# Attention and two mixture-of-experts layers on one core: the first layer in three token passes instead of four

## The chip, the core and the metric

The program runs on one core of a Trainium2 chip. The core has five engines with instruction queues of their own: TensorE (PE; its weight loads are shown apart as PEld), VectorE (DVE), ScalarE (ACT), GpSimd (POOL) and SyncE (SP, which here only issues transfers). They meet through semaphores. The metric is the device time of one launch in microseconds, lower is better. Before the change it is 1419.59 us, the median of 3 runs (1416.87 to 1421.7).

## What is computed

Four batches of 576 tokens go through block-causal attention with 8 heads, then through two feed-forward layers. All is float32, cut here to what matters:

```python
# attention: q, k, v are (4 batches, 8 heads, 576 tokens, 64)
scores = q @ k.T / 8, masked where block_of(query) < block_of(key)   # blocks of 64
x = softmax(scores) @ v                          # -> (2304 tokens, 512)
# first layer ("moe1"): w_gate, w_val (512, 1536), w_out (1536, 512)
x = (1 / (1 + exp(-(x @ w_gate))) * (x @ w_val)) @ w_out
# second layer ("moe2"): 4 experts, w1 (512, 1024), w2 (1024, 512) each
p = domain_probs / (sum(domain_probs) + 1e-9)
out = sum over e of p[:, e] * (relu(x @ w1[e]) @ w2[e])
```

## The kernel before

**Precision and products.** A float32 operand is split in two fp32r tiles, a high part (made on ACT) and a remainder (made on DVE or POOL), and each product is three matmuls: high by high, high by low, low by high. On top of that the products with `w_gate`/`w_val` and `w1` are done in seven block products instead of eight, over two token halves `t`, two column blocks and two halves of the contraction. The sums that this needs are prepared by POOL: for the tokens in `winograd_left` (tiles `xs`, then seven tiles `xc1[1]` to `xc1[7]`), for the weights in `conv_items` (tiles `wa` to `wd`).

**First layer.** The 2304 tokens are taken in passes; before the change four passes of one batch each (`NP1`, `TP1`), so that each matmul streams half a pass, `TH1` = 288 token columns. In a pass a loop runs over 12 slices `f` of 128 of the 1536 hidden columns. For each `f`, `l1_1` does seven products of six matmuls each in two PSUM banks, `c1` and `c2`: ACT copies partial sums out (`snap`), DVE adds them up (`total`), the gate is made by ACT and DVE, and the result is split in the tile `g`. For each two slices, `l2_1` multiplies `g` with `w_out` (tile `wo`), into bank `lo`: 4 blocks `dm` of 128 output columns by 2 token halves, each group 6 matmuls in a row; ACT or DVE adds the group to the tile `x2[t, dm]`, and after the last two slices it is written to DRAM (`x2_d`). A pass has 12 x (42 + 24) = 792 matmuls. The products `l1_1` of two slices and `l2_1` of the two slices before them are merged in one list by cost.

**Weights.** They come as 64-bit floats. In the stretch before the first pass and in pass 0, `conv_items` and `wo_get` convert and split them (ACT, DVE and POOL) and write the split form to DRAM; every later pass loads it again, per slice 4 transfers for `wa` to `wd` and one for `wo`.

**Attention** is a list of items (`attn_items`) put in between: `attn_to` advances it while the first layer runs, to a place set by `A1` and `PACE1`. Batches 0 and 1 ("N") use plain float32 matmuls, 2 and 3 ("F") the split form. Each pair of heads of a batch gives two DRAM tiles: `xd..a`, tokens 0 to 255, and `xd..b`, tokens 256 to 575. They are read back by `x1_prep` or `x1_early` to make the seven token tiles of a pass. While attention runs it owns the PSUM banks `s`, `t` and `o`; from pass 2 on, where it is over, `m_bank` gives the first layer these too, so each of `c1`, `c2` and `lo` has two banks, and the gate is a plain sigmoid.

**Second layer.** Three passes of 768 tokens (`TH` = 384 columns per matmul). In its pass 0 the second matmul has 512 columns, in passes 1 and 2 it is again in seven products, with 256 columns. Its first weights (`w_prep`, `w_load`, `w2_load`) and first token tiles (`x_prep(0)`) are made during the last pass of the first layer.

**Order.** The program is emitted in the order of these lists; a scheduler then moves instructions within each engine by a timeline of its own, and a pool's `bufs` number says how many tiles of a name live at once. SP carries all large transfers in one queue, in order.

Of the kernel before, what the change touches and what calls it, by code (L numbers as in the profile page):

```python
# [21 lines left out]
A1 = [1.05, 2.3, 4, 4, 4]  # L22
PACE1 = 0.9
GB = 4
UB = 1
# [9 lines left out]
W2B = 4  # L35
FIRSTP = 1
W1B = 5
PRE0, PRE1 = 0.4, 0.9
# [24 lines left out]
def attention_moe_moe_kernel(  # L63
# [72 lines left out]
    moe1 = tc.alloc_tile_pool(name="moe1", bufs=1)  # L136
# [15 lines left out]
    def attn_items(segs):  # L152
# [6 lines left out]
        QTS = KTS = {"N": range(5), "F": range(5)}  # L159

        def nat_of(g):
            return pairs[g][3] != "F"
# [20 lines left out]
        def load(g, nm, src, c0, c1):  # L183
# [14 lines left out]
            for x, (y, z) in enumerate(((nm, src),) if nm == "v" else (("k", k), ("q", q)) if nm == "k" else ()):  # L198
                nc.sync.dma_start(
                    out=t[64 * x:64 * x + 64, 4], in_=z[b, 2 * pr:2 * pr + 2, 512:S, :].rearrange("h p d -> p h d"))  # L200
# [6 lines left out]
        def loads(g):  # L207
            load(g, "q", q, 0, 4)
# [61 lines left out]
        first = sum(x[3] != "F" for x in pairs)  # L270
# [4 lines left out]
        for g, pair in enumerate(pairs):  # L275
# [3 lines left out]
            if pair[3] == "F":  # L279
# [10 lines left out]
        order = {"N": 0, "F": 0}  # L290
# [251 lines left out]
        def prep_list(g):  # L542
            seg = pairs[g][3]
            r = [(False, 0.0, lambda: prep_alloc(g))]
            for nm, cs in (("q", range(4)), ("k", KTS[seg])):
# [12 lines left out]
        for g in range(len(pairs)):  # L558
# [5 lines left out]
            later(base + per // 2, (g, False, 0.0, lambda g=g: load_v(g)))  # L564
# [47 lines left out]
    NP1 = B  # L612
    TP1 = S
    TH1 = TP1 // 2
    QF = 2 * P
    KH = NKT // 2
    C1 = TH1 / 2.4 + 2.6
# [3 lines left out]
    wo_d = [dram.tile([P, 2, DM], F32, name=f"wod{i}") for i in range(NF)]  # L621
# [3 lines left out]
    def w1_tile(k):  # L625
        n = 1 if k == "d" else 2
        return moe1.tile([P, 2, n, QF], F32R, tag="wd" if k == "d" else "wg", name=f"w{k}", bufs=2 if k == "d" else 6)
# [48 lines left out]
    def wo_get(p, f):  # L676
        t = wo[f] = moe1.tile([P, 2, DM], F32R, tag="wo", name="wo", bufs=4)
        if p:
            nc.sync.dma_start(out=t.bitcast(F32), in_=wo_d[f])
# [3 lines left out]
        split_sb(t[:, 0], t[:, 1], from_f64(raw), "a", "p")  # L683
        nc.sync.dma_start(out=wo_d[f], in_=t.bitcast(F32))
# [18 lines left out]
    def winograd_left(pool, dst, load, n):  # L703
# [7 lines left out]
        def s(kk, m):  # L711
            if m in (1, 3):
                d[kk, "s", m] = pool.tile([P, n], F32, tag=f"xs{m}", name="xs")
# [22 lines left out]
    def x1_prep(p):  # L736
        def load(kk, t, h):
            kt = h * KH + kk
            r = moe1.tile([P, TH1], F32, tag="xr1", name="xr1", bufs=4)
            while (p, "b", kt) not in x_d:  # L740
                attn_next()
            if t == 0:
                nc.sync.dma_start(out=r[:, :QA], in_=x_d[p, "a", kt])
# [690 lines left out]
```

## Time and profile before

| | us |
|---|---|
| median of 3 runs | 1419.59 (1416.87 to 1421.7) |
| the profiled execution | 1417.34 |
| its span, first to last instruction | 1415.6 |
| busy in the span: PE / DVE / ACT / POOL | 1373.8 / 983.1 / 780.7 / 480.4 |
| attention alone with weight conversion | 0 to about 117 |
| first layer, passes 0 and 1, attention beside them | about 117 to 470 |
| first layer, passes 2 and 3 | about 470 to 680.5 |
| second layer, passes 0, 1, 2 | 680.5 to 930, to 1160, to 1415.6 |

The span is what one execution shows on the engines; 1.7 us lie around it. A matmul's own duration in the profile contains the way through the array, which the next one overlaps, so what a matmul costs in a stream is read from the distance of starts, not from its duration.

### The profile page before, as it was taken

To read this page: it belongs to the slowest core of one execution; us is meant where nothing else is said; L and a number is where in the kernel's file an instruction comes from. 1 tells how busy PE (TensorE), PEld (TensorE's weight loads), DVE (VectorE), ACT (ScalarE), POOL (GpSimd) and SP (SyncE) were. 2 spreads that over 40 slices of the span, in tenths; PEclk is the share of its full clock that TensorE was granted. 3 is DMA by queue.
4 is the path that set the end of the run, shared out by engine and by line. 5 is a ranking of instruction groups with operands and counts; after the bars stand their busy time and mean duration, and the time that the engine had idled before them with its cause. 6 is when DMAs were issued, how large, how long until landed. Compare 5 with 4: busy or idle time off the path is not lost.

```text
span 1415.6 us, 26232 instructions
## 1 busy us (share of the span) xinstructions
PE 1373.8 (97%) x9212; PEld 1266.7 (89%) x9212; DVE 983.1 (69%) x2103; ACT 780.7 (55%) x1926; POOL 480.4 (34%) x502
## 2 busy tenths in 40 slices
PE   5889999999999999999999999999999999999998
PEld 3447788889899999999999989989999999999998
DVE  6867789986766445467777666757766687766766
ACT  5878788888876433343445445445444454443442
POOL 4544345312112100012576556533322342322322
PEclk8989999999999999999999999999999999999999
DMA  7988787767756888898799888886676777676754
GB/s 227 311 243 277 218 278 264 246 204 214 217 178 229 306 296 267 282 364 311 264 336 358 296 300 302 281 308 227 226 254 249 249 266 278 246 269 231 276 205 157
DMA packets 213683, 371.93 MB, mean 263 GB/s; under 512 B 75568, under 2 KB 140080, under 8 KB 207408
## 3 DMA queue, kind: packets, MB, share of 16 engines
q1 hardware_dynamic: 212464, 369.99, 77.1%
q8 instruction: 74, 1.21, 0.3%
q14 instruction: 57, 0.47, 0.1%
q10 hardware_dynamic: 1088, 0.26, 0.1%
HBM read 269.00 MB, written 101.19 MB: 262 GB/s over the span
## 4 chain that ended last, share of the span: by engine, by line
PE 83%; DMA 5%; DVE 5%; ACT 3%; issue 2%; SPq 1%; POOL 1%; DVEq 0%; ACTq 0%; POOLq 0%
PE c L119 37%; PE o L119 25%; PE lo L119 7%; PE s L119 4%; PE obank L119 3%; PE t L119 2%; PE tbank L458 2%; DMA raw<-in_moe_w_out_dram 1%; DMA raw<-in_moe_w_gate_dram 1%; PE s L349 1%; DMA wa<-w1d 1%; ACT pt L382 1%; DMA w1g<-w1d 1%; PE tbank L229 1%; POOL wt L653 1%
## 5 line engine op out<-in xcount | busy, mean ns | idle before, releaser
L119 PE MATMUL c<-xc,w1g 128*128 128x384 f32 x1920 | 384.8, 338 | 2.1 <-DMA w1g<-w1d 1.8
L119 PEld LDWEIGHTS c<-xc,w1g 128*128 128x128 f32 x1920 | 330.4, 188 | 8.8 <-DVE hb L1062 1.3
L119 PE MATMUL o<-w2s,hb 128*128 128x256 f32 x1728 | 243.5, 282 | 1.1 <-DVE acc L1211 1.1
L119 PEld LDWEIGHTS o<-w2s,hb 128*128 128x128 f32 x1728 | 231.8, 189 | 2.0 <-DVE acc L1211 1.7
L1211 DVE SCALAR_TENSOR_TENSOR acc<-o,pr_t,acc 128x256 f32<-128x256 f32 x264 | 123.4, 479 | 57.9 <-PE o L119 55.7
L1071 POOL TENSOR_TENSOR hs<-hf 128x384 f32<-128x384 f32 x64 | 64.1, 1023 | 287.1 <-ACT hf L1079 255.7
L119 PE MATMUL lo<-g,wo 128*128 128x288 f32 x888 | 148.0, 300 | 4.8 <-DVE x L884 4.8
L119 PE MATMUL o<-w,hb 128*128 128x512 f32 x576 | 142.9, 391 | 0.0
L119 PEld LDWEIGHTS lo<-g,wo 128*128 128x128 f32 x888 | 125.8, 188 | 9.6 <-DVE x L884 6.7
L1079 ACT ACTIVATE hf<-c 128x384 f32<-128x384 f32 x128 | 65.7, 513 | 115.7 <-DVE c L1116 58.4
L119 PEld LDWEIGHTS o<-w,hb 128*128 128x128 f32 x576 | 107.2, 188 | 18.5 <-DVE acc L1155 0.3
L1116 DVE TENSOR_TENSOR c<-c,snap 128x384 f32<-128x384 f32 x144 | 77.9, 553 | 55.8 <-PE c L119 38.9
L1109 ACT ACTIVATE snap<-c 128x384 f32<-128x384 f32 x144 | 65.8, 485 | 85.6 <-PE c L119 85.4
L1060 ACT ACTIVATE hb<-hs 128x384 fp32r<-128x384 f32 x128 | 63.3, 518 | 65.0 <-POOL hs L1071 64.9
L1062 DVE TENSOR_TENSOR hb<-hs,hb 128x384 fp32r<-128x384 f32 x128 | 87.1, 695 | 5.8 <-ACT hb L1060 5.4
L884 DVE TENSOR_TENSOR x<-lo,x 128x288 f32<-128x288 f32 x124 | 55.6, 452 | 45.6 <-PE lo L119 45.0
L119 PE MATMUL c<-xc,wa 128*128 128x288 f32 x504 | 82.6, 299 | 0.9 <-DMA wa<-w1d 0.5
L382 ACT ACTIVATE pt<-s,nm 128x128 f32<-128x128 f32 (+3 forms) x128 | 67.4, 530 | 17.2 <-DVE nm L380 14.5
L119 PEld LDWEIGHTS c<-xc,wa 128*128 128x128 f32 x504 | 71.2, 188 | 3.1 <-DMA wa<-w1d 0.8
L119 PE MATMUL c<-xc,wc 128*128 128x288 f32 x432 | 71.0, 299 | 1.1 <-ACT snap L808 1.1
L458 PE MATMUL tbank<-ident,pt 128*128 128x128 f32 x320 | 55.3, 287 | 17.2 <-ACT pTa L445 9.9
L808 ACT ACTIVATE snap<-c 128x288 f32<-128x288 f32 x108 | 44.2, 409 | 43.8 <-PE c L119 43.2
(173 smaller groups left out, 2697.5 us busy)
## 6 DMA issues: line engine op xcount, KB each, us to landing
w1g<-w1d SPq DMA_DIRECT2D x96, 512.0 KB, 5.4
w2s<-w2d SPq DMA_DIRECT2D x48, 1024.0 KB, 6.5
w1d<-w1g SPq DMA_DIRECT2D x48, 512.0 KB, 5.0
wa<-w1d SPq DMA_DIRECT2D x40, 512.0 KB, 5.2
wb<-w1d SPq DMA_DIRECT2D x40, 512.0 KB, 5.3
wc<-w1d SPq DMA_DIRECT2D x40, 512.0 KB, 4.4
wo<-wod SPq DMA_DIRECT2D x36, 512.0 KB, 6.0
wr<-in_moe_w_dram SPq DMA_DIRECT2D x32, 512.0 KB, 5.4
```

Of the source, the lines that this page charges most:

```text
L119: ins = nc.tensor.matmul(out=out, lhsT=lhsT, rhs=rhs, start=start, stop=stop, skip_group_check=skip)
L382: ins = nc.scalar.activation(out=pt[:, x * nk:(x + 1) * nk], in_=sp[:, x - x0], func=AF.Exp, bias=nm[:, j0 + x:j0 + x + 1], scale=1.0, acc ...
L458: nc.tensor.transpose(out=tbank[:, x * P:(x + 1) * P], in_=pt[:, x * P:(x + 1) * P], identity=ident)
L808: nc.scalar.activation(out=t, in_=d["c1"][:, :TH1], func=AF.Copy)
L884: nc.vector.tensor_tensor(out=x2[t, dm], in0=ps, in1=x2[t, dm], op=ALU.add)
L1060: nc.scalar.activation(out=t[:, 0], in_=src, func=AF.Copy if low is None else AF.Relu)
L1062: nc.vector.tensor_tensor(out=t[:, 1], in0=src, in1=t[:, 0].bitcast(F32), op=ALU.subtract)
L1071: nc.gpsimd.tensor_tensor(out=o, in0=x, in1=y, op=op)
L1079: nc.scalar.activation(out=hf[q, blk], in_=c, func=AF.Relu)
L1109: nc.scalar.activation(out=t, in_=d["c1"][:, :TH], func=AF.Copy)
L1116: nc.vector.tensor_tensor(out=c, in0=d[tag][:, :TH], in1=d[n], op=ALU.add)
L1211: nc.vector.scalar_tensor_tensor(out=o, in0=ps, scalar=pr, in1=o, op0=ALU.mult, op1=ALU.add)
```

## The change

The first layer takes three passes, of 576, 832 and 896 tokens, so that its matmuls stream 288, 416 and 448 columns. That has consequences in three places.

*Tokens.* Pass 1 consists of batch 1 and the first 256 tokens of batch 2, pass 2 of the rest of batch 2 and batch 3 (table `X1`). So that the first 256 tokens of batch 2 are there in time, the attention of batch 2 is two segments, "G" (query tiles 0 and 1 of every head pair) and "H" (tiles 2 to 4); key tiles 0 and 1 are loaded and transposed in both. `A1` and `PACE1` place batch 1 and G in pass 0, H and batch 3 in pass 1. The two-bank form holds for the last pass only.

*Space.* The one pool `moe1` becomes pools per pass (`mg`, `mx`, `my`) and one for the weights (`wts`), released and opened again between passes. There are 5 weight tiles instead of 6 (`WGB`), `wo` comes in halves of which 6 are held (3 whole ones, 4 before), 2 `snap` tiles instead of 3 (`SNB`). Raw token loads and sums use tiles that the gate uses later (`room`). `l2_1` goes over `dm` first and the token half second.

*Seams.* After pass 0 its last `l2_1` list is emitted before anything of pass 1 (`go(prev, [])`). The token tiles of pass 2 lie where attention lay, and are made during the last two slices of pass 1 (`XE`). At the end of the first layer one part of the weights of slice 0 of the second layer and all weights of its slice 1 are prepared after the last `l2_1` list (`run(wp[0][6:7] + wp[1])`); before, all but three parts were made inside the last pass.

```diff
-A1 = [1.05, 2.3, 4, 4, 4]
-PACE1 = 0.9
+A1 = [1.05, 3.05, 5, 5]
+PACE1 = (1.0, 0.9, 0.9)
+WGB = 5
+WOB = 6
+SNB = 2
+XE = 2
...
-        QTS = KTS = {"N": range(5), "F": range(5)}
+        QTS = {"N": range(5), "F": range(5), "G": range(2), "H": range(2, 5)}
+        KTS = {"N": range(5), "F": range(5), "G": range(2), "H": range(5)}
...
-    NP1 = B
-    TP1 = S
-    TH1 = TP1 // 2
+    N1 = (288, 416, 448)
+    O1 = (0, 576, 1408)
+    NP1 = len(N1)
+    X1 = (((0, "a", 0, 256), (0, "b", 0, 32)), ((0, "b", 32, 320),)), \
+         (((1, "a", 0, 256), (1, "b", 0, 160)), ((1, "b", 160, 320), (2, "a", 0, 256))), \
+         (((2, "b", 0, 320), (3, "a", 0, 128)), ((3, "a", 128, 256), (3, "b", 0, 320)))
...
     def x1_prep(p):
+        n = N1[p]
+        keep = {}
+
+        def room(key, m):
+            if key not in keep:
+                pool, tag = (xst, key[0]) if p == 2 else (my[p], key[0])
+                keep[key] = pool.tile([P, m, n], F32, tag=tag, name="xr1", bufs=dict(c=2, snap=SNB).get(tag, 1))
+            return keep[key]
...
+            for b, g, c0, c1 in X1[p][t]:
+                while (b, g, kt) not in x_d:
+                    attn_next()
+                nc.sync.dma_start(out=r[:, o:o + c1 - c0], in_=x_d[b, g, kt][:, c0:c1])
+                o += c1 - c0
...
         def snap(n):
-            t = d[n] = moe1.tile([P, TH1], F32, tag="snap", name="snap", bufs=3)
+            t = d[n] = my[p].tile([P, n1], F32, tag="snap", name="snap", bufs=SNB)
...
-        for t in (1, 0):
-            for dm in range(NKT):
+        for dm in range(NKT):
+            for t in (1, 0):
...
-                    pre = x_prep(0) + [...] + wp[0] + wp[1][:-2] + [...]
+                    pre = x_prep(0) + [...] + wp[0][:6] + wp[0][7:] + [...]
...
+                    if p == 1 and f >= NF - XE:
+                        if f == NF - XE:
+                            attn_to(99)
+                            xcp[2] = tc.alloc_tile_pool(name="xc2", bufs=1, side="right", reuse_waits="tile")
+                            xst = tc.alloc_tile_pool(name="xst", bufs=1, side="right", reuse_waits="tile")
+                            xi = x1_prep(2)
+                        x0 = f - (NF - XE)
+                        side += [x for _, x in xi[len(xi) * x0 // XE:len(xi) * (x0 + 1) // XE]]
...
                 prev = l2_1(p, f0)
+                if f0 == NF - 2 and p < NP1 - 1:
+                    my[p].release()
+                    mx[p].release()
+                    if p == 0:
+                        go(prev, [])
+                        prev = []
+                        mg[0].release()
...
         run(prev)
         ps1.release()
-        moe1.release()
-        p2 = tc.alloc_tile_pool(name="p2", bufs=1, reuse_waits="tile")
+        mg[2].release()
+        xcp[2].release()
+        wts.release()
+        p2 = tc.alloc_tile_pool(name="p2", bufs=1, side="right", reuse_waits="tile")
         ps2 = tc.alloc_tile_pool(name="ps2", bufs=1, space=PSUM, reuse_waits="tile")
+        hb_first = [p2.tile([P, 2, TH], F32R, tag="hb", name="hb", bufs=HB)]
         w2_load(1)
+        run(wp[0][6:7] + wp[1])
```

**TensorE between pass 0 and pass 1.** `lo` is the bank of `l2_1`, `c_..` a bank of `l1_1`, `xc_..` a token tile, `tbank`, `s` and `obank` are attention. Before, where the first products of pass 1 (`xc_3697`, `xc_3705`) begin:

```order
L478 MATMUL tbank<-ident,pt_4093 128x128 x4
L119 MATMUL lo<-g,wo 128x288 x6
L119 MATMUL c_3754<-xc_3697,wa 128x288 x6
L119 MATMUL c_3808<-xc_3705,wa 128x288 x3
L119 MATMUL s<-tk,tq 128x128
```

And of the change, the same place (pass 1 has 416 columns):

```order
L512 MATMUL tbank<-ident,xr 128x128 x2
L514 MATMUL tbank<-ident,nm 128x128
L124 MATMUL c_4008<-xc_3952,wa 128x416 x3
L124 MATMUL c_4044<-xc_3960,wa 128x416 x3
L124 MATMUL c_4008<-xc_3952,wa 128x416
L124 MATMUL lo<-g,wo 128x288 x6
L124 MATMUL c_4044<-xc_3960,wa 128x416
```

In both, products of pass 1 stand between the last groups of pass 0. In the change the first two products are cut in pieces of 3, 1 and 2 matmuls, each of which waits for a part of the token tiles, and seven more `lo` groups of pass 0 and the attention of batch 2 follow before the third product.

**ScalarE at the start of the second layer.** `w_9286`, `w_9306` and `w_8203`, `w_8211` are the high parts of the first two down-projection weights, made from raw tiles `wr_..`; `snap` frees a partial sum of the first products; before:

```order
L1109 ACTIVATE snap<-c_9269 128x384
L912 ACTIVATE w_9286<-wr_9089 128x512
L912 ACTIVATE w1g<-wt 128x512
L912 ACTIVATE w_9286<-wr_9089 128x512
L1121 ACTIVATE hb<-c 128x384
L1109 ACTIVATE snap<-c_9339 128x384
L912 ACTIVATE w_9306<-wr_9267 128x512 x2
L1109 ACTIVATE snap<-c_9269 128x384
```

And of the change:

```order
L920 ACTIVATE w1g<-wt 128x512
L920 ACTIVATE w1g<-wr_7798 128x512
L1139 ACTIVATE snap<-c_8194 128x384
L920 ACTIVATE w_8203<-wr_7988 128x512 x2
L1151 ACTIVATE hb<-c 128x384
L920 ACTIVATE w_8211<-wr_8167 128x512 x2
L1139 ACTIVATE snap<-c_8257 128x384
L1139 ACTIVATE snap<-c_8194 128x384
```

Two weight copies for slices 0 and 1 stand ahead of the first `snap`, and both later `snap` copies stand behind `w_8211`; before, one of them stood ahead of `w_9306`.

**TensorE at the same place.** The bank `c_9269` (`c_8194` in the change) is used by the first product, and again by three later ones of the same slice, each of which waits for a `snap`; before:

```order
L119 MATMUL c_9269<-xc_8150,w1g 128x384 x6
L119 MATMUL c_9294<-xc_8239,w1g 128x384 x6
L119 MATMUL c_9316<-xc_8221,w1g 128x384 x6
L119 MATMUL c_9339<-xc_8150,w1g 128x384 x6
L119 MATMUL c_9428<-xc_8221,w1g 128x384 x6
L119 MATMUL c_9269<-xc_8270,w1g 128x384 x6
L119 MATMUL c_9378<-xc_8239,w1g 128x384 x6
L119 MATMUL c_9269<-xc_8339,w1g 128x384 x6
```

And of the change:

```order
L124 MATMUL c_8194<-xc_7107,w1g 128x384 x6
L124 MATMUL c_8219<-xc_7152,w1g 128x384 x6
L124 MATMUL c_8246<-xc_7138,w1g 128x384 x6
L124 MATMUL c_8257<-xc_7107,w1g 128x384 x6
L124 MATMUL c_8194<-xc_7238,w1g 128x384 x6
L124 MATMUL c_8296<-xc_7152,w1g 128x384 x6
L124 MATMUL c_8194<-xc_7267,w1g 128x384 x6
```

The third use of that bank is the eighth product before and the seventh now.

Over the whole program the change has 792 matmuls fewer in the first layer and 8 transposes of keys more.

## Rows read from the trace of the kernel before

**Rows 1.** The page: busy time and share of the span by engine.

```profile
PE 1373.8 (97%) x9212; PEld 1266.7 (89%) x9212; DVE 983.1 (69%) x2103; ACT 780.7 (55%) x1926; POOL 480.4 (34%) x502
```

**Rows 2.** The page: the chain of work that ended last, by engine.

```profile
PE 83%; DMA 5%; DVE 5%; ACT 3%; issue 2%; SPq 1%; POOL 1%; DVEq 0%; ACTq 0%; POOLq 0%
```

**Rows 3.** Stretches: PE, PEld, DVE, ACT, POOL busy (instructions); clock, DMA, GB/s.

```profile
207.00:297.00 90.00, 84.02 (x605) 73.98 (x603) 82.90 (x201) 76.78 (x212) 38.67 (x39) 1.00 0.79 254
297.00:440.00 143.00, 142.67 (x1059) 128.79 (x1060) 97.27 (x290) 113.05 (x320) 24.50 (x38) 1.00 0.64 194
...
470.00:575.00 105.00, 104.71 (x790) 104.48 (x789) 53.53 (x106) 37.70 (x86) 2.43 (x2) 1.00 0.81 278
575.00:682.00 107.00, 106.32 (x797) 105.83 (x797) 65.67 (x134) 40.68 (x98) 18.51 (x18) 1.00 0.87 310
```

**Rows 4.** Timeline of PE: start, length, matmuls of one width in a row.

```profile
674.94 5.72 PE L119 MATMUL lo<-g,wo 128*128 128x288 f32 x42
680.50 10.75 PE L119 MATMUL c<-xc,w1g 128*128 128x384 f32 x60
...
782.42 4.28 PE L119 MATMUL o<-w,hb 128*128 128x512 f32 x18
786.54 2.27 PE L119 MATMUL c<-xc,w1g 128*128 128x384 f32 x12
788.65 1.53 PE L119 MATMUL o<-w,hb 128*128 128x512 f32 x6
...
1060.44 1.58 PE L119 MATMUL o<-w2s,hb 128*128 128x256 f32 x12
1061.86 1.22 PE L119 MATMUL c<-xc,w1g 128*128 128x384 f32 x6
```

**Rows 5.** Whom PE waited for, 117 to 297: total us, times, longest.

```profile
PE lo L119 <- DVE x L884: 4.4, 5, 1.4
```

**Rows 6.** Whom PE waited for, 470 to 682.

```profile
PE c L119 <- DMA wa<-w1d: 0.5, 1, 0.5
PE s L119 <- DMA wa<-w1d: 0.3, 1, 0.3
PE s L119 <- DMA wc<-w1d: 0.2, 1, 0.2
```

**Rows 7.** Groups by form: count | busy us, mean ns | idle before, releaser.

```profile
L229 PE MATMUL tbank<-ident,kn 128*128 128x128 f32 x80 | 15.6, 296 | 1.1 <-ACT tqn L237 0.5 <-ACT pTb L445 0.5
L884 DVE TENSOR_TENSOR x<-lo,x 128x288 f32<-128x288 f32 x124 | 55.6, 452 | 45.6 <-PE lo L119 45.0
L1116 DVE TENSOR_TENSOR c<-c,snap 128x384 f32<-128x384 f32 x144 | 77.9, 553 | 55.8 <-PE c L119 38.9 <-ACT snap L1109 16.5
L131 ACT ACTIVATE xc<-xr 128x384 fp32r<-128x384 f32 x18 | 8.9, 518 | 8.9 <-DMA xr<-x2d 6.1 <-PE c L119 2.8
L718 POOL TENSOR_TENSOR xs<-xr 128x384 f32<-128x384 f32 x12 | 13.5, 1125 | 140.4 <-DMA xr<-x2d 114.9 <-DVE xc L133 17.2 <-DVE x L884 8.3
L133 DVE TENSOR_TENSOR xc<-xs,xc 128x384 fp32r<-128x384 f32 x24 | 14.0, 584 | 7.3 <-ACT xc L131 7.2
```

**Rows 8.** Timeline of PE where pass 1 begins; idle before in brackets.

```profile
294.26 0.40 PE L119 MATMUL c<-xc,wa 128*128 128x288 f32 x1 [0.20 <-ACT xc L131]
...
297.28 0.66 PE L458 MATMUL tbank<-ident,pt 128*128 128x128 f32 x4 [0.81 <-ACT pTb L445]
```

**Rows 9.** Timeline of ACT as the second layer begins.

```profile
686.23 1.15 ACT L912 ACTIVATE w<-wr 128x512 fp32r<-128x512 f32 x2 [0.81 <-DMA wr<-in_moe_w_dram]
687.29 0.47 ACT L1109 ACTIVATE snap<-c 128x384 f32<-128x384 f32 x1
```

**Rows 10.** Timeline of SP: the last attention output goes to DRAM.

```profile
440.73 0.32 SPq L540 DMA_DIRECT2D xd3b<-xr  x1
```

**Rows 11.** Timeline of PE: the first product of pass 2.

```profile
458.37 0.29 PE L119 MATMUL t<-xc,wb 128*128 128x288 f32 x1
```

**Rows 12.** Tile `xd3b`, its writes and reads: time from issue to landing.

```profile
DMA to landing us min/median/max: 1.8/4.5/7.0
```

More of the change, by code (lines that the diff above doesn't have):

```diff
@@ L268, in last_q @@
                     out=w[64:128, r], in0=src[r], scalar=SCALE, in1=w[0:64, r].bitcast(F32), op0=ALU.mult, op1=ALU.subtract)
-        first = sum(x[3] != "F" for x in pairs)
+        first = sum(x[3] == "N" for x in pairs)
         seq, start = [], []
@@ L289, in attn_items @@
         st = {}
-        order = {"N": 0, "F": 0}
+        order = dict.fromkeys("NFGH", 0)
         ring = []
@@ L676, in wo_get @@
     def wo_get(p, f):
-        t = wo[f] = moe1.tile([P, 2, DM], F32R, tag="wo", name="wo", bufs=4)
+        ts = wo[f] = [wts.tile([P, 2, QF], F32R, tag="wo", name="wo", bufs=WOB) for _ in range(2)]
         if p:
-            nc.sync.dma_start(out=t.bitcast(F32), in_=wo_d[f])
+            for x, t in enumerate(ts):
+                nc.sync.dma_start(out=t.bitcast(F32), in_=wo_d[f][:, x])
             return
@@ new lines, in load @@
+            if p == 2:
+                r = room(("xr", kk), 4)[:, 2 * t + h]
+            elif kk == 0:
+                r = room(("c", t), 2)[:, h]
+            elif t == 0:
+                r = room(("r",), 2)[:, h]
+            else:
+                r = room(("snap", h), 1)[:, 0]
+            o = 0
+            for b, g, c0, c1 in X1[p][t]:
[3 more added lines that the diff above has]
+                o += c1 - c0
@@ L783, in attention_moe_moe_kernel, with sums @@
+            return r
+        def sums(kk, m):
+            return room(("xs" if p == 2 else "t", kk), 2)[:, int(m == 3)]
+        if p == 1:
+            for m in (3, 4, 7, 6, 2, 5, 1):
+                xc1.setdefault(p, {})[m] = xcp[p].tile([P, 2, KH, n], F32R, tag=f"xc{m}", name=f"xc{m}")
+        return winograd_left(xcp[p], xc1.setdefault(p, {}), load, sums, n)
     gs = {}
@@ L925, in load, with sums, w1_room @@
                 return a
-            return winograd_left(p2r, xc, load, TH)
+            def sums(kk, m):
+                if p:
+                    return p2.tile([P, TH], F32, tag=f"xs{m}", name="xs")
+                if (kk, "s") not in keep:
+                    keep[kk, "s"] = p2r.tile([P, 4, QF], F32, tag="wt", name="xs").rearrange("p a d -> p (a d)")
+                x = int(m == 3)
+                return keep[kk, "s"][:, x * TH:(x + 1) * TH]
+            return winograd_left(p2r, xc, load, sums, TH)
+        w1n = [0]
+        def w1_room():
+            w1n[0] += 1
+            x = (w1n[0] - 1) % W1B
+            pool, n = (p2r, W1P) if x < W1P else (p2, W1B - W1P)
+            return pool.tile([P, 2, 2, QF], F32R, tag="w1g", name="w1g", bufs=n)
         wq = {}
```

180 lines of the change are left out of this document (75 added, 105 removed).

## Prediction

> **What bounds the kernel now.** I read the page's busy times first: PE is busy 97% of the span, DVE 69%, ACT 55% [rows 1]. The chain that ended last is PE's own work for 83%, with 5% each for transfers and DVE [rows 2]. So a change must shorten PE's stream or the waits in it. A table of stretches then shows where waits are: the reader is to subtract PE's busy time from the length. From 470 to 682, passes 2 and 3 of the first layer, PE is idle 0.29 + 0.68 = 1.0 us of 212; from 297 to 440, pass 1 with attention, 0.3 of 143; but from 207 to 297, the end of pass 0, 6.0 of 90, and there DVE is busy 82.9 of 90 [rows 3]. The list of waits names the cause: `lo` groups waited 4.4 us for DVE's additions into `x` [rows 5]. The clock is at its upper level, 2.4 GHz, in all these stretches (granted 1.00), and nothing in the change empties PE for long; I expect it to stay.
>
> **The sum** is made against the profiled execution, 1417.34 us (span 1415.6), which lies 2.25 us under the median of the runs shown, 1419.59; the forecast is given on the median.
>
> *Fewer, wider matmuls.* The token columns streamed are the same: 3168 matmuls of 288 before, 792 each of 288, 416 and 448 after, 912,384 columns both times. What can be saved is what a matmul costs beyond its columns. From starts in the timeline [rows 4]: 42 of 288 columns in 680.50 - 674.94 = 5.56 us, 132.4 ns each; 18 of 512 in 4.12 us, 228.9 ns; 12 of 384 in 2.11 us, 175.8 ns; 12 of 256 in 1.42 us, 118.3 ns. At 2.4 GHz the columns take 120.0, 213.3, 160.0 and 106.7 ns, so 12.4, 15.6, 15.8 and 11.7 ns are left over. 416 and 448 do not occur. If they leave 12.4 ns as 288 does, 792 matmuls fewer save 9.8 us. If they lie on the line from 384 to 512, they take 189.1 and 202.4 ns, the three passes take 792 x (132.4 + 189.1 + 202.4) = 414.9 us instead of 419.5, and 4.6 us are saved. The runs of 384 and 512 stand in the second layer, beside more work on the other engines; I take the middle, -7.2.
>
> The Trainium skill has a rule on this (TensorE: Matmul & The Clock Gate, section Back-to-back issue gap): a warm matmul starts N / 2.4 + 2.5 ns after the one before. By it 792 matmuls are worth 2.0 us, as an estimate from that page of the Trainium skill. The trace has 12 to 16 ns where the page has 2.5, so it does not agree; but the rule speaks for the rival of no gain below.
>
> *Work added by G and H.* Eight transposes of keys: the 80 there are take 15.6 us, 195 ns each [rows 7], so 1.6 us if nothing hides them, 0 if they fall in a wait; with 16 evictions on ACT and 8 subtractions on DVE, which stand beside PE's work: +1.3.
>
> *Waits that go.* Passes 2 and 3 become one. Of their 1.0 us of idle time, all is for weight loads [rows 6]; a slice now lasts 66 x 202.4 = 13.4 us instead of 66 x 132.4 = 8.7, with the same transfers, so I count that as gone. In passes 0 and 1, an addition into `x` costs 452 ns for 288 columns, a like DVE addition 553 ns for 384 [rows 7]: 1.05 ns per column, and 149 ns per instruction that a wider pass has less often. Pass 0 keeps its width, but part H of batch 2, part of which stood in it, comes after it. Of the 6.0 us at its end I take 1.5 away. Together -2.5; the ends are 0 and -7.0.
>
> *Seam of pass 0 and 1.* Now PE stands 0.20 + 0.81 us there [rows 8]. In the change no other product of the first layer than two of pass 1 stands among the last eight `lo` groups of pass 0; attention does. All eight use one bank, so each waits for DVE's addition to the one before, 0.45 us, while ACT and DVE also make 14 splits of 416 columns, 0.52 us (ACT) and 0.58 us (DVE) each at 384 [rows 7]. On ACT that is over 7 us in a stretch where the eight groups take 8 x 0.79 = 6.4 us of PE and attention about as much. Lower end: the 1.0 us that stand there now go. Upper end: every group waits as long as the longest wait of pass 0, 1.4 us [rows 5], 11.2 us. I take +2.2, twice what stands there now: the space of the first token tiles (`xc_3952`, `xc_3957`) was the converter's, so their making need not wait for pass 0.
>
> *Seam of pass 1 and 2.* Pass 2 now needs batch 3, where before it needed batch 2. The chain is a write and a read of DRAM, 4.5 us each at the median and 7.0 at most [rows 12], a sum on POOL, a split on ACT and DVE (1.1 + 0.5 + 0.6 us [rows 7]): 11.2 us, at most 16.2. In the order, 18 groups of six matmuls of 416 columns stand between the last attention product and the first of pass 2: 20.4 us. (Before, 17.6 us passed between [rows 10, 11].) Covered: 0. SP, which issues the reads, has weight loads behind them, and these have a slice's time of slack.
>
> *Start of the second layer.* All weights of slice 1 are now split there. DVE does those after its last addition into `x`; the fourth product needs them 3 x 1.06 us after the start, DVE has two splits before it: covered. On ACT two `snap` copies stand behind `w_8211`, which waits for its load. Before, that pair of copies began at 686.23, 5.7 us after the second layer's first matmul, behind a wait, and the next `snap` began at 687.29 [rows 4, 9]. It was needed by the eighth product, due 7 x 1.06 = 7.4 us after the start, and done at 7.3. Now two copies come behind it, done at about 7.8, and the seventh product is due at 6.4: +1.4. Ends: 0, if the load comes 1.5 us earlier, and +3.
>
> With the fourth pass its weight loads go too; beyond the 1.0 us above PE does not wait for such loads in passes 2 and 3: 0.
>
> Sum: -7.2 + 1.3 - 2.5 + 2.2 + 1.4 = -4.8 us: 1412.5 for the profiled execution, 1414.8 on the median, and I say 1414.5. Adding the ends: -9.8 - 7.0 - 1.0 = -17.8 and -4.6 + 1.6 + 11.2 + 3 = +11.2.
>
> **Rivals.**
> A, *more gain*: 207 to 297 is bound by DVE (82.9 of 90), not by PE; then the first layer's work under attention grows by 256 tokens while attention takes as long as before, and the added work fills idle time. Visible are 6.0 us there. With 9.8 us from the matmuls and no seam: 1419.6 - 9.8 - 6.0 + 1.3 = 1405. For it: DVE at 92%. Against: from 297 to 440 PE has no idle time left to fill.
> B, *no gain from width*: the time per column is nearly the same at all widths (118.3 / 256 = 0.462, 132.4 / 288 = 0.460, 175.8 / 384 = 0.458), as if the rest grew with the columns. Then the first term is 0, the others stay: 1419.6 + 2.4 = 1422; with the seams at half, 1420. By the rule of the Trainium skill named above (TensorE: Matmul & The Clock Gate, Back-to-back issue gap) the matmuls give 2.0 us and the time is 1420. Against: 512 columns have 0.447.
> C, *slower*: the seam of pass 0 and 1 is set by DVE and ACT. If DVE is as full there as from 207 to 297, each of the eight `lo` groups waits 1.4 us and the token tiles come last: +11.2 there, +3 at the second layer, against -7.2: 1419.6 + 11.2 + 3 + 1.6 - 7.2 = 1428. It decides from a seam of about 9 us up. For it: only attention is left to fill PE, and attention waits for ACT too. Against: in the stretch behind the seam before, DVE was busy 97 of 143.
>
> **Chances.** Forecast 0.50 (1409 to 1418), A 0.17, B 0.20, C 0.13. A measurement tells 0.3%, 4.3 us, from no change. Below 1415.3 lie A and about 0.38 of the forecast's 0.50; within 4.3 us the other 0.12 and most of B (0.17), above 1423.9 C and 0.03 of B, rounded: faster 0.55, same 0.29, slower 0.16. Range: 1403 to 1424, which takes in A and B and leaves out C and the far end of A.
>
> **What would show it.** Runs of 416 and 448 columns spaced 187 to 190 and 200 to 203 ns (185.8 and 199.1 would give the full 9.8 us; 191 and 206 none). PE's idle time and the `lo` waits at the last eight groups of 288 columns: 3 us or less; 9 or more is C. The first 448-column product with no wait for the tiles. The seventh product of the second layer 1 to 2 us late behind ACT. The forecast is wrong if a stall of more than 4 us stands at any seam, or if passes 0 and 1 gain more than 5 us over the sum of their matmuls.

## The result and the profile after

The changed kernel takes 1440.74 us (median of 4 runs, 1438.99 to 1442.48) against 1419.87 for the kernel before (4 runs beside it): ratio 1.0149, 95% interval 1.0128 to 1.0171. It is 21 us slower; 1414.5 was predicted, with a range to 1424. The profiled execution took 1442.48 us, its span is 1440.7.

The page of the changed kernel, busy time by engine and the chain by engine. PE is busy 8.4 us longer than before, with the same token columns in its first layer; its share has fallen by one point only, as the span grew by 25.1 us. PE's part of the chain fell from 83% to 76% [rows 1, 2]: DVE, transfers and ACT now end more of it.

```profile
PE 1382.2 (96%) x8428; PEld 1247.8 (87%) x8428; DVE 983.7 (68%) x2011; ACT 784.8 (54%) x1874; POOL 486.0 (34%) x514
PE 76%; DVE 8%; DMA 7%; ACT 4%; issue 3%; POOL 1%; SPq 1%; DVEq 0%; ACTq 0%; POOLq 0%
```

Where the 25.1 us arise: the first product of the second layer started at 680.50 [rows 4] and now starts at 700.43 (timeline of PE), so in these two profiles 19.9 us are lost before it and 5.2 behind it.

```profile
697.75 2.84 PE L124 MATMUL lo<-g,wo 128*128 128x448 f32 x13
700.43 6.46 PE L124 MATMUL c<-xc,w1g 128*128 128x384 f32 x36
708.05 2.00 PE L124 MATMUL c<-xc,w1g 128*128 128x384 f32 x10 [1.16 <-ACT snap L1139]
```

A single profile tells this to some 4 us only. The run with `PACE1 = 0.92` below has the same order as the kernel before on PE, ACT, DVE and POOL; in its profile the second layer starts at 676.6 and lasts 737.7 us, against 680.5 and 735.1. Over all profiles the second layer lasts 736.5 to 740.2 us in the seven kernels with the change, 738.6 in the mean, and 733.6 to 738.6 in the eleven that leave it as it was before, 735.3 in the mean: some 3 us are lost behind its start, not 5.

Stretches of the kernel before that are not shown ahead of the prediction (stretch, length, busy time of PE, PEld, DVE, ACT, POOL, then clock, share of DMA, GB/s):

```profile
70.00:117.00 47.00, 41.03 (x252) 25.20 (x252) 32.05 (x90) 35.42 (x108) 21.57 (x24) 0.89 0.81 243
117.00:207.00 90.00, 87.67 (x614) 71.33 (x613) 70.01 (x175) 74.39 (x209) 33.23 (x35) 1.00 0.80 257
312.00:350.00 38.00, 37.95 (x286) 34.89 (x285) 28.89 (x87) 33.70 (x99) 6.72 (x10) 1.00 0.78 231
450.00:575.00 125.00, 124.40 (x934) 123.65 (x933) 69.19 (x132) 51.44 (x114) 9.55 (x7) 1.00 0.83 289
```

And the same stretches of the changed kernel, with 207 to 297 [rows 3] and the last pass:

```profile
70.00:117.00 47.00, 38.80 (x229) 23.68 (x230) 30.05 (x87) 32.68 (x100) 19.38 (x23) 0.89 0.71 211
117.00:207.00 90.00, 83.14 (x573) 65.02 (x574) 66.15 (x162) 69.80 (x205) 29.99 (x32) 1.00 0.72 228
207.00:297.00 90.00, 83.15 (x581) 74.21 (x581) 79.25 (x181) 74.23 (x199) 47.90 (x48) 0.98 0.82 260
312.00:350.00 38.00, 34.73 (x207) 28.95 (x208) 30.78 (x82) 30.76 (x85) 6.07 (x7) 1.00 0.67 187
450.00:575.00 125.00, 122.44 (x652) 111.63 (x651) 69.50 (x120) 63.67 (x127) 15.04 (x17) 1.00 0.63 197
575.00:700.00 125.00, 125.00 (x606) 113.56 (x605) 67.06 (x107) 40.98 (x75) 12.91 (x12) 1.00 0.56 176
```

The reader is to look at the first two rows of each block. All three of PE, DVE and ACT do less there than before, 4.5, 3.9 and 4.6 us less from 117 to 207: no engine has become the bound, they wait for each other. That stretch is pass 0, whose matmuls kept their width. The list of PE's waits from 117 to 297 says for what: products and transposes of attention (`s`, `tbank`) waited 8.1 us for ACT and DVE, where they had waited 1.4 before, while the `lo` groups waited less. The two longest of these lines:

```profile
PE s L124 <- ACT pt L392: 2.0, 2, 1.1
PE tbank L468 <- DVE tq L256: 1.4, 1, 1.4
```

The last row above has no idle time: the pass of 448 columns runs clean.

### The profile page after: what moved, and what is told of

It reads as the page before. It is cut to its first block, busy times and chain, and to the rows that moved or that the text cites. A ratio compares the mean times of both kernels' runs of the same rounds, so it can differ in the third digit from the quotient of the medians.

```text
span 1440.7 us, 24459 instructions
## 1 busy us (share of the span) xinstructions
PE 1382.2 (96%) x8428; PEld 1247.8 (87%) x8428; DVE 983.7 (68%) x2011; ACT 784.8 (54%) x1874; POOL 486.0 (34%) x514
## 4 chain that ended last, share of the span: by engine, by line
PE 76%; DVE 8%; DMA 7%; ACT 4%; issue 3%; POOL 1%; SPq 1%; DVEq 0%; ACTq 0%; POOLq 0%
PE c L124 35%; PE o L124 24%; PE lo L124 7%; PE s L124 3%; PE obank L124 2%; PE t L124 2%; DMA raw<-in_moe_w_val_dram 2%; PE tbank L468 1%; DVE raw L618 1%; PE s L359 1%; DVE raw L617 1%; ACT pt L392 1%; DVE nm L390 1%; DMA raw<-in_moe_w_out_dram 1%; DMA out_dram<-acc 1%
## 5 line engine op out<-in xcount | busy, mean ns | idle before, releaser
L124 PE MATMUL lo<-g,wo 128*128 128x288 f32 (+2 forms) x744 | 154.3, 341 | 5.5 <-DVE x L892 5.3
L124 PE MATMUL c<-xc,wa 128*128 128x288 f32 (+2 forms) x396 | 81.5, 341 | 3.0 <-DVE xc L138 1.7
L892 DVE TENSOR_TENSOR x<-lo,x 128x288 f32<-128x288 f32 (+2 forms) x104 | 56.0, 543 | 41.2 <-PE lo L124 40.8
L815 ACT ACTIVATE snap<-c 128x288 f32<-128x288 f32 (+2 forms) x90 | 43.3, 481 | 56.8 <-PE c L124 52.3
L124 PE MATMUL c<-xc,wc 128*128 128x288 f32 (+2 forms) x360 | 73.7, 340 | 0.0
L124 PEld LDWEIGHTS c<-xc,wa 128*128 128x128 f32 x396 | 66.5, 188 | 8.2 <-DVE xc L138 2.2
```

Of the source, the lines that this page charges most:

```text
L124: ins = nc.tensor.matmul(out=out, lhsT=lhsT, rhs=rhs, start=start, stop=stop, skip_group_check=skip)
L815: nc.scalar.activation(out=t, in_=d["c1"][:, :n1], func=AF.Copy)
L892: nc.vector.tensor_tensor(out=x2[t, dm], in0=ps, in1=x2[t, dm], op=ALU.add)
```

## The experiments

Ratios are to the kernel before on the same chip, with 95% intervals. "End of layer 1" is the start of the first product with `w1g` in the profiled execution, 680.5 before and 700.4 in the changed kernel; it too is told to some 4 us. The kernel before took 1416.5 to 1419.9 us on the chips of these runs, so where a time lies near the end of an expected range I go by the ratio times 1419.87.

**The rooms of pass 0, together.** "Rooms" are buffers. In the first run pass 0 of the changed kernel gets its buffers back (the code for the halves of `wo` and for the sums is left out here):

```diff
+        if k != "d" and in0[0]:            # in pass 0, every 6th weight tile
...
+            return conv.tile([P, 2, n, QF], F32R, tag="wg0", name=f"w{k}")
...
+            if p == 0:
+                r = my[0].tile([P, n], F32, tag="xr1", name="xr1", bufs=4)
...
-... name="snap", bufs=SNB)
+... name="snap", bufs=3 if p == 0 else SNB)
```

> The changed kernel with the buffers of the kernel before given back in the stretch before pass 0 and in pass 0 only: a sixth weight tile, 8 halves of wo, 3 snap tiles, and raw token tiles and sums of their own. Passes 1 and 2 stay as changed. The profile of the changed kernel loses about 20 us before the second layer, 6 before 117 us, 7 from 117 to 200 and 7 from 200 to 312. Theory R (rooms): the engines wait for buffers there, POOL up to 17.6 us for one weight tile; then most of 13 to 20 us comes back, 1421 to 1428. Theory G (the split attention of batch 2 costs more on ACT and DVE): nothing comes back, 1438 to 1442. Theory O (the order the scheduler arrives at, by chance): anything from 1425 to 1445, without a relation to the waits for buffers.

Measured 1438.49 us, ratio 1.0146 (1.0130 to 1.0162): nothing came back. The stretches say why:

```profile
207.00:297.00 90.00, 85.37 (x612) 75.78 (x611) 79.34 (x187) 76.45 (x207) 39.47 (x42) 1.00 0.81 259
312.00:350.00 38.00, 32.86 (x177) 23.79 (x177) 29.04 (x87) 31.59 (x91) 13.52 (x17) 0.87 0.49 131
```

From 207 to 297 PE does 2.2 us more than in the changed kernel, but at the seam 1.9 us less, at a granted clock of 0.87 instead of 1.00. The last slice of pass 0 begins 14.3 us earlier than in the changed kernel (273.3 instead of 287.6), and the first product of pass 1 6.4 us later (315.7 instead of 309.3): a pass 0 that is ahead gives nothing if the next seam takes it back. By the order in which the pools are opened the added tiles lie where token tiles of pass 1 go; no trace shows that this is the reason. The mirror image, the kernel before with the small rooms:

```diff
-... tag="wg" ... bufs=2 if k == "d" else 6)
+... tag="wg" ... bufs=2 if k == "d" else 5)
-... tag="wo", name="wo", bufs=4)
+... tag="wo", name="wo", bufs=3)
-... tag="snap", name="snap", bufs=3)
+... tag="snap", name="snap", bufs=2)
...
+            if kk == 0:   r = room(("c", t), 2)[:, h]
+            elif t == 0:  r = room(("r",), 2)[:, h]
+            else:         r = room(("snap", h), 1)[:, 0]
```

> The mirror image: the kernel before with the changed kernel's buffers, 5 weight tiles, 3 whole wo tiles, 2 snap tiles, and the raw token tiles and sums of passes 0 and 1 in the gate's tiles. Four passes of 288 columns as before. Theory R: 13 to 20 us slower, 1433 to 1440, with the loss before 300 us. Theory G: no change beyond 3 us, 1417 to 1423. Theory O: somewhere in 1415 to 1435.

Measured 1452.45 us, 1.0245 (1.0224 to 1.0265), 34 us and so twice the expected loss. A part of it is not that of the changed kernel: from 450 to 700 PE waited 7.5 us for loads of `wo`, of which only three whole tiles are held here, where the changed kernel holds six halves and its own list of waits has no such line. Three `wo` tiles alone were not tried.

```profile
PE lo L119 <- DMA wo<-wod: 7.5, 6, 2.2
```

The first run again, with the added tiles in the converter's space and only up to slice 8 of pass 0:

```diff
-                r = my[0].tile([P, n], F32, tag="xr1", name="xr1", bufs=4)
+                r = conv.tile([P, n], F32, tag="xr1", name="xr1", bufs=4)
...
+                    if (p, f) == (0, 8):   # from here the changed kernel's rooms
+                        items.append((0.0, lambda: in0.__setitem__(0, False)))
```

> The changed kernel with pass 0's buffers given back as in the first run, but laid in the space of the converter, so that the gate tiles keep their place, and only up to slice 8 of pass 0 (a sixth weight tile, two more halves of wo, a third snap tile; raw token tiles and sums of their own). In the first run pass 0 ended some 15 us earlier and the stretch 312 to 350 lost 14 us at the seam. Theory R+S (rooms cost about 16 us in the prologue and pass 0, and the first run only lost them again at the seam because the extra tiles stood where the token tiles of pass 1 go): 1422 to 1429. Theory S alone (whatever pass 0 gains, the seam takes back, since pass 1 waits for something that comes at about 315 to 340 us anyhow): 1435 to 1441.

Measured 1433.20 us, 1.0105 (1.0080 to 1.0131). About 6 us come back of the 16 that I ascribed to the rooms, so R+S is too large. Theory S alone (the seam takes back whatever pass 0 gains) is not excluded: the ratio stands for 1434.8 us, 1431.2 to 1438.5, and S said 1435 to 1441.

**The rooms one by one.** In the kernel before, one at a time: `bufs=6` to `5` for the weights, `bufs=3` to `2` for `snap`, and the `room` lines above, which take in the tokens of passes 0 and 1.

> The kernel before with 5 weight tiles instead of 6, nothing else. If this room carries the loss of pass 0 (POOL waits up to 17.6 us for one in the changed kernel): 8 to 15 us slower, 1427 to 1434. If the snap or the token tiles carry it: within 3 us, 1416 to 1422.

Measured 1422.34 us, 1.0023 (1.0006 to 1.0040): a small cost.

> The kernel before with 2 snap tiles instead of 3, nothing else. The third snap of a slice then waits for DVE's addition of the first; ACT stands behind it, and PE behind ACT. If this room carries the loss: 8 to 15 us slower, 1427 to 1434, spread over all four passes. Otherwise within 3 us, 1416 to 1422.

Measured 1418.69 us, 1.0007 (0.9993 to 1.0021): none.

> The kernel before with the raw token tiles and sums of passes 0 and 1 in the tiles of the gate (c, r, snap, t) as in the changed kernel, nothing else. If this carries the loss: 5 to 10 us slower, 1424 to 1429, all of it at the start of pass 0 (70 to 120 us) and at the seam of pass 0 and 1. Otherwise within 3 us, 1416 to 1422.

Measured 1430.15 us, 1.0084 (1.0054 to 1.0115), end of layer 1 at 690.8. Of the three it is the only large cost. What it does in the changed kernel is seen on PE at the first slice:

```profile
73.92 0.64 PE L124 MATMUL c<-xc,wa 128*128 128x288 f32 x3
78.00 0.40 PE L124 MATMUL c<-xc,wa 128*128 128x288 f32 x1 [0.15 <-ACT xc L136]
80.08 0.54 PE L124 MATMUL c<-xc,wa 128*128 128x288 f32 x2 [1.68 <-DVE xc L138]
80.45 0.38 PE L239 MATMUL tbank<-ident,kn 128*128 128x128 f32 x2
...
129.17 1.86 PE L124 MATMUL c<-xc,wa 128*128 128x288 f32 x12 [0.89 <-DVE c L818]
```

The kernel before:

```profile
72.35 0.64 PE L119 MATMUL c<-xc,wa 128*128 128x288 f32 x3
76.00 0.44 PE L229 MATMUL tbank<-ident,kn 128*128 128x128 f32 x2 [0.18 <-ACT pTb L445]
...
91.70 0.38 PE L119 MATMUL c<-xc,wa 128*128 128x288 f32 x1
92.51 0.53 PE L119 MATMUL c<-xc,wa 128*128 128x288 f32 x2
...
122.84 1.86 PE L119 MATMUL c<-xc,wa 128*128 128x288 f32 x12
```

With four raw tiles in a ring the second token block comes late, and its products stand late in PE's order. With the gate's tiles its first raw tile is there at once; the order puts its product at 78, the next ones wait there for their split, and the key transposes (`kn`) of attention, which went at 76 before, stand behind them until 80.45. ACT's split of a sum of the first block comes 6.5 us later than before; the changed kernel, then the kernel before:

```profile
98.40 0.77 ACT L136 ACTIVATE xc<-xr 128x288 fp32r<-128x288 f32 x2
```

```profile
91.94 0.43 ACT L131 ACTIVATE xc<-xs 128x288 fp32r<-128x288 f32 x1
```

POOL's next sum waits until DVE has made the remainder for this split; the changed kernel, then the kernel before:

```profile
101.42 0.92 POOL L735 TENSOR_TENSOR xr<-xr,xr 128x288 f32<-128x288 f32 x1 [10.39 <-DVE xc L138]
```

```profile
92.97 0.79 POOL L718 TENSOR_TENSOR xs<-xs,xr 128x288 f32<-128x288 f32 x1 [3.52 <-DVE xc L133]
```

The second slice begins 6.3 us late, at 129.17. But two other traces speak against this chain as the cause of the loss. In the kernel before with this edit alone the key transposes go at 76.20 as before, and the second slice is as late all the same:

```profile
76.20 0.44 PE L229 MATMUL tbank<-ident,kn 128*128 128x128 f32 x2
...
129.00 1.04 PE L119 MATMUL c<-xc,wa 128*128 128x288 f32 x6
```

And in the changed kernel with `A1[0] = 1.12`, a run further below, the product waits in the same place and the key transposes come at 78.66, but the second slice is in time, while the whole kernel is no faster (ratio 1.0158):

```profile
78.29 0.55 PE L124 MATMUL c<-xc,wa 128*128 128x288 f32 x2 [1.15 <-DVE xc L138]
...
122.28 1.86 PE L124 MATMUL c<-xc,wa 128*128 128x288 f32 x12
```

So an early second slice does not carry through to the end of layer 1, and how the sharing of tiles costs time stays open. Now the undoing, alone, in the changed kernel:

```diff
+            if p == 0:
+                r = conv.tile([P, n], F32, tag="xr1", name="xr1", bufs=4)
...
+            if p == 0:
+                return conv.tile([P, n], F32, tag=f"xs{m}", name="xs")
```

> The changed kernel with raw token tiles and sums of pass 0 in tiles of their own (in the converter's space), nothing else: the single undoing of what cost 0.84% alone in the kernel before. If the sharing with the gate's tiles is half of the loss there too: 1428 to 1433. If it only cost because of the third room or the sixth weight tile beside it: 1436 to 1441.

Measured 1434.56 us, 1.0116 (1.0090 to 1.0141): some 5 us back, which lies between the two expected ranges and, by the ratio (1436.3 us), in the one for a sharing that costs only beside the other rooms. The interval overlaps that of the changed kernel (1.0128 to 1.0171). The second slice begins at 122.38 and layer 1 ends at 692.5, 7.9 us earlier. All rooms together (1433.20) gave hardly more. Only the sharing in pass 0 is undone here; that in pass 1 was not tried in the changed kernel.

```profile
122.38 2.00 PE L124 MATMUL c<-xc,wa 128*128 128x288 f32 x12
```

**The split attention.** The kernel before with segments G and H:

```diff
-        queue = attn_items([(0, "N"), (1, "N"), (2, "F"), (3, "F")])
+        queue = attn_items([(0, "N"), (1, "N"), (2, "G"), (2, "H"), (3, "F")])
-A1 = [1.05, 2.3, 4, 4, 4]
+A1 = [1.05, 3.08, 5, 5, 5]
```

> The kernel before with the attention of batch 2 in two segments (query tiles 0 and 1 of all head pairs, then tiles 2 to 4) and the same place in the planner's list at the end of pass 0 (3.08 instead of 2.3, by the list's costs). All else as before. Theory G: the eight extra key transposes with their evictions and the eight short preparations bring DVE and ACT, already 92% and 85% busy at the end of pass 0, over the edge: 10 to 20 us slower, 1430 to 1440, lost between 200 and 300 us. Theory R: 1 to 3 us slower, 1420 to 1423, the price of 8 transposes. Theory O: 1415 to 1435.

Measured 1422.66 us, 1.0041 (1.0027 to 1.0055); end of layer 1 at 688.7. A cost, below what theory G (the split loads ACT and DVE) expected. Two variants, one with places weighted by cost:

```diff
+            w = {2: 0.24, 3: 0.76}.get(x, 1.0)
+            place += [x - 0.76 * (x > 2) - 0.24 * (x > 3) + w * sum(costs[:i]) / sum(costs) ...]
```

> The kernel before with batch 2's attention in two segments, as in the third run (which was 0.4% slower), but with the planner's places weighted by cost: batch 1 counts 1.0, the first segment of batch 2 0.24, the second 0.76, so that pass 0 calls attention at the same rate as in the kernel before (1.05 to 2.3). In the third run each segment counted 1.0, so that batch 1's attention was called for in the first 0.42 of pass 0 instead of the first 0.68, and the short first segment over the next 0.44. Theory P (the uneven rate costs): back to 1417 to 1420. Theory G (the splitting itself, with its 8 more preparations and short chains, costs): stays at 1422 to 1426.

Measured 1424.66 us, 1.0052 (1.0034 to 1.0069): theory P (the uneven rate of attention costs) falls. The same weights in the changed kernel with its tokens apart:

> The kernel of the run before this one, and the planner's places weighted by cost as in the first of these runs (pass 0 from 1.05 to 2.28 of 4). Theory P: 3 to 7 us less than the run before this one, 1423 to 1429. Theory G: the same within 2 us.

Measured 1434.08 us, 1.0113 (1.0090 to 1.0135), equal to the kernel without them. The other variant has each pair's H right behind its G:

```diff
+        queue = attn_items([(0, "N"), (1, "N"), (2, "GH"), (3, "F")])
+        pairs = [... for pr in range(NPAIR) for y in seg]
```

> The kernel before with batch 2's attention split, but each pair's second segment right behind its first one, so that the order of batch 2 is by pairs as before: the same added work as in the third run (8 key transposes, 16 evictions, 8 subtractions, loads of keys and values twice), without the run of four short segments in a row. Theory W (the added work costs): 5 to 8 us slower, as the two kernels with all first segments in front, 1422 to 1426. Theory N (four short segments in a row starve PE, since each has few products to cover its preparation): 0 to 3 us slower, 1417 to 1421. Theory O: no relation.

Measured 1427.02 us, 1.0071 (1.0048 to 1.0093): theory N (four short segments in a row starve PE) falls. The three kernels roughly fit theory W (the added work costs), but also the next group.

**The order alone.** The kernel before, with the planner's numbers moved and nothing else:

> The kernel before with one number of the planner moved a little, PACE1 from 0.90 to 0.92, which changes no work and no buffer, only at which item the attention is advanced. Theory O: the order is sensitive, the time moves by 4 to 15 us either way. Theories R and G: within 3 us, 1417 to 1423.

Measured 1417.59 us, 0.9994 (0.9982 to 1.0007). The order had stayed the same on PE, ACT, DVE and POOL, so this run is a repetition and tests no theory. With `A1 = [1.00, 2.3, 4, 4, 4]`, and then 1.12 in place of 1.00:

> The kernel before with one planner's number moved, A1[0] from 1.05 to 1.00: a little less attention is called before pass 0. The work and all buffers are the same; the order on PE, ACT and DVE differs from early in the prologue on (PACE1 = 0.92, run earlier, turned out to leave the order as it was, so that run was only a repetition). Theory O (the order that the scheduler arrives at is worth 5 to 10 us by itself): off the kernel before by more than 4 us either way. Theories R and G: within 3 us, 1415 to 1421.

> The same with A1[0] = 1.12. Theory O: off by more than 4 us, in either direction, and not by the same as the run before this one. Theories R and G: within 3 us, 1415 to 1421.

Measured 1429.03 us, 1.0066 (1.0050 to 1.0083), and 1428.10 us, 1.0061 (1.0046 to 1.0077). The same work on the same buffers is 9 us slower, both ways, and layer 1 ends at 690.4 and 692.0 (timelines of PE, 1.00 and 1.12):

```profile
690.42 10.73 PE L119 MATMUL c<-xc,w1g 128*128 128x384 f32 x60
```

```profile
692.00 10.78 PE L119 MATMUL c<-xc,w1g 128*128 128x384 f32 x60
```

In the kernel with 1.00, PE's waits from 200 to 460 are other ones than in the kernel before, where `lo` for DVE led the list in pass 0 [rows 5]:

```profile
PE c L119 <- DVE r L811: 2.5, 3, 1.2
PE c L119 <- ACT snap L808: 2.0, 2, 1.1
PE tbank L229 <- DVE tq L246: 1.2, 1, 1.2
PE lo L119 <- DVE x L884: 1.2, 3, 0.6
```

So the order is worth up to 0.66% here, about as much as each split kernel lost: the split cannot be told from the new order that comes with it. Nor can the sharing of token tiles (1.0084), whose interval overlaps that of the run with 1.00. Not every new order costs that much, though: with 5 weight tiles the order also differs from early in the prologue on, at 0.23%. The same number moved in the changed kernel:

```diff
-A1 = [1.05, 3.05, 5, 5]
+A1 = [1.00, 3.05, 5, 5]    # and 1.12
```

> The changed kernel with A1[0] from 1.05 to 1.00, the number that alone made the kernel before 0.66% slower by another order of the same work. Theory D (the kernel before stands at an order that its number happens to fit, and the changed kernel, with other tiles and pools, is a draw at the same number): the time moves either way by 3 to 10 us, and may come down to 1431. Theory F (the changed kernel's order is as well fitted as that of before, so that its whole 1.5% comes from its parts): slower by 5 to 10 us, 1446 to 1451. If its loss comes from waits for buffers that no order removes: within 3 us, 1438 to 1444.

> The changed kernel with A1[0] = 1.12, the number that alone made the kernel before 0.61% slower. The same theories: D either way by 3 to 10 us; F 1446 to 1451; waits that no order removes 1438 to 1444. If both draws come out below 1440, about 6 to 9 us of the change's loss are the lost fit and not its parts.

Measured 1435.31 us, 1.0133 (1.0119 to 1.0146), and 1439.45 us, 1.0158 (1.0142 to 1.0173), beside 1.0149. Theory F (the changed kernel's order is as well fitted as the other's) is out: neither neighbour is slower by 5 to 10 us. D's wide spread is not seen either; neither ratio can be told from 1.0149. By the ratios the two stand for 1438.8 and 1442.3 us, in the range of waits that no order removes. In time both lie below 1440, the mark set for a lost fit, but on a chip on which the kernel before is 3.3 us faster (1416.53), so I don't count it as met.

**The start of the second layer.** The kernel before with the late preparation, and then also with three of the five weight tiles in the pool opened late:

```diff
-... + wp[0] + wp[1][:-2] + [(0.0, lambda: w2_load(0))]
+... + wp[0][:6] + wp[0][7:] + [(0.0, lambda: w2_load(0))]
+        run(wp[0][6:7] + wp[1])
# second kernel also:
+            pool, n = (p2r, W1P) if x < W1P else (p2, W1B - W1P)
```

> The kernel before with the one change at the start of the second layer: the third pair of weights of its slice 0 and all weights of its slice 1 are prepared after the last product list of the first layer. In the changed kernel the second layer lasts 740.3 us instead of 735.1; its 42nd product matmul comes at 8.8 us instead of 7.4 and its 97th at 34.3 instead of 29.6. If that part of the change carries it: 3 to 5 us slower, 1420 to 1424, all of it in the first 35 us of the second layer. If it is the space (tiles on other sides, weights in two pools): within 1.5 us, 1416 to 1420.

> The kernel before with the late preparation of the second layer's first weights (alone no change: ratio 1.0004) and, as in the changed kernel, only two of the five pair tiles in the pool that is open during the last pass and three in the pool that is opened after it, in the space of the first layer's tiles. If that space is the cause of the second layer's lost 3 to 5 us: 1420 to 1424, with the seventh product about 1 us late and the second slice's products 4 to 6 us late at first. If it is the other tiles there (raw tokens and sums in the weights' tiles): within 1.5 us, 1416 to 1420.

Measured 1419.00 us, 1.0004 (0.9990 to 1.0019), and 1419.85 us, 1.0003 (0.9992 to 1.0013). The second shows the changed kernel's pattern. ACT and PE of the second kernel, then ACT of the changed kernel:

```profile
686.62 1.15 ACT L913 ACTIVATE w<-wr 128x512 fp32r<-128x512 f32 x2 [2.55 <-DMA wr<-in_moe_w_dram]
687.67 0.85 ACT L1118 ACTIVATE snap<-c 128x384 f32<-128x384 f32 x2
```

```profile
680.57 6.48 PE L120 MATMUL c<-xc,w1g 128*128 128x384 f32 x36
688.58 4.59 PE L120 MATMUL c<-xc,w1g 128*128 128x384 f32 x24 [1.52 <-ACT snap L1118]
```

```profile
706.09 1.15 ACT L920 ACTIVATE w<-wr 128x512 fp32r<-128x512 f32 x2 [2.17 <-DMA wr<-in_moe_w_dram]
707.14 0.85 ACT L1139 ACTIVATE snap<-c 128x384 f32<-128x384 f32 x2
```

Both `snap` copies stand behind a weight split that waits for its load, and the seventh product waits for them. So the space explains the pattern, and the pattern costs at most 1.9 us of the whole, by the upper end of the interval. In this kernel's profile the second layer lasts 1418.3 - 680.6 = 737.7 us, 2.6 more than before, but the repetition with the old order lasts as long. What makes up the rest of the some 3 us there, the shared tiles among other things, was not tried.

## Why the prediction was wrong, step by step

**Width, -7.2: mis-sized.** The six matmuls of 416 columns and of 448 columns are read from one timeline of the changed kernel:

```profile
562.62 1.29 PE L124 MATMUL lo<-g,wo 128*128 128x416 f32 x6
563.75 0.57 PE L124 MATMUL o<-g,wo 128*128 128x448 f32 x2
...
570.24 1.40 PE L124 MATMUL c<-xc,wa 128*128 128x448 f32 x6
571.48 1.20 PE L124 MATMUL t<-xc,wb 128*128 128x448 f32 x5
```

They take (563.75 - 562.62) / 6 = 188.3 ns and (571.48 - 570.24) / 6 = 206.7 ns, where I had put 187 to 190 and 200 to 203. With 288 at 132.4 the three passes take 792 x 527.4 = 417.7 us instead of 419.4: 1.7 us saved. Rival B had this right: 416 and 448 columns leave over more than 288 do. The Trainium skill (TensorE: Matmul & The Clock Gate, Back-to-back issue gap) gives N / 2.4 + 2.5 ns, for an isolated matmul; 2.0 us follow from it, as an estimate. Its gap does not agree with the trace (12.4 to 20.0 ns over the columns, not 2.5, and not constant), so that 2.0 lies near the measured 1.7 is luck.

**"Pass 0 keeps its width, but part H of batch 2 ... comes after it": the step that failed.** From it I took the prologue and pass 0 as they were, less 1.5 us of `lo` waits. Those waits did fall by 1.5 (2.9 us in 7 waits from 117 to 297, 4.4 in [rows 5]), and it did not matter: PE's idle time from 207 to 297 went from 6.0 to 6.9 us, and from 117 to 207 from 2.3 to 6.9. What grew are attention's waits for ACT and DVE, to 8.1 us. I never costed the edits that reach pass 0 through space: raw tokens in the gate's tiles (12 us alone in the kernel before, some 5 back when undone in pass 0 of the changed one), 5 weight tiles (3 us). Nor did I give the order itself a range, though the pieces of the order ahead of the prediction showed that it changes; alone it is worth 9 us in the kernel before. A term was missing rather than mis-sized: even the upper ends of my sum together, +11.2, give 1430.8. And neither of my signs of being wrong came, no stall of 4 us at a seam and no large gain in passes 0 and 1, since I had named none for a loss there.

The clock did not quite stay either. Once in pass 0 the granted clock fell to its lower level, 1.2 GHz, for 3.4 us, behind a stretch (272 to 279.6) in which PE had been idle for 2.1 of 7.6 us. At half speed that costs at most 1.7 us.

```profile
279.60:283.00 3.40, 3.40 (x15) 3.38 (x16) 2.44 (x8) 2.57 (x7) 1.30 (x2) 0.50 0.56 204
```

**Transposes of G and H, +1.3.** The split as a whole measured 0.41 to 0.71%, 6 to 10 us, but in kernels with a new order; its own work can't be read from these.

**Seam of pass 0 and 1, +2.2: right in size, in part by luck.** PE is idle 3.3 us from 312 to 350, where 1.0 us stood at the seam before [rows 8]: +2.3. Two `lo` groups waited there, against rival C's eight; as long a wait, for a load of attention's keys, was in no term of mine (PE's waits, 312 to 350):

```profile
PE tbank L239 <- DMA kn<-in_k_dram: 1.3, 1, 1.3
PE lo L124 <- DVE x L892: 1.3, 2, 0.9
```

C's total (1428) came nearest, by a mechanism that is not there.

**Seam of pass 1 and 2, 0: nearly.** The first 448-column product (519.76) waited for nothing. From 450 to 575 PE idles 2.6 us (0.6 before), for DVE's gate and `lo` additions. Attention ends at 491 instead of 440, so more of pass 1 runs beside it.

**Start of the second layer, +1.4: right for the product named.** The seventh product came 708.05 - 700.43 = 7.62 us after the layer's start, against 6 x 1.06 = 6.36 in the unbroken run before [rows 4]: 1.3 late, behind ACT as said. The layer as a whole takes some 3 us more over all profiles; what adds the rest isn't shown.

Adding up the profiles for layer 1: split with its order 8.2 to 9.9 (688.7 and 690.4 in two of the kernels), tokens 7.9, seam of pass 0 and 1 2.3, width -1.7, together 16.7 to 18.4 of 19.9. These overlap, since each edit also makes a new order, and each mark is told to some 4 us, so the sum is a guide and no proof.

**What stays open.** The cause of the loss is shown in part at most. Open are how much of the split's cost and of the token tiles' is work or waiting and how much is order; and whether the kernel before stands at a fitted point (both neighbours cost it 9 us, while the changed kernel moves by some 2, which can't be told from nothing). Not tried alone are the new sequence inside `l2_1`, `wo` in halves, the pace of 1.0 in pass 0 and the pools per pass. No kernel tried beats the kernel before by more than the measurement tells.

## What to carry to other kernels

When a scheduler derives the order, a stretch whose instructions are the same is not a stretch whose time is the same: move a number that changes no work, and take the spread (here 9 us of 1419) as a term of the range before summing terms of 2 us. A late instruction that a trace shows is not yet the cause: look for a trace in which it comes in time, and see whether the kernel gains. Here the second slice came 7 us earlier in one run and the kernel was no faster. Before reading a few microseconds out of two profiles, take the profile of a repetition. And measure a matmul's spacing at the very widths of the change; a line between two others was 4 ns off.

## What the runs showed of the hardware

At a granted clock of 1.00, beyond its columns at 2.4 GHz a matmul left over 12.4 ns at 288 columns, 15.8 at 384 and 15.6 at 512 [rows 4], and 15.0 at 416 and 20.0 at 448 in the lines above: not constant, and not a line.

Two executions of one order started the second layer 3.9 us apart (680.5 and 676.6), though their spans were 1415.6 and 1414.3 us: here the parts of a profile varied more than its sum.
